# A third score room in the products' two PSUM banks for the first 28 tiles, and the first heads' attended values in the transposes' banks

## The chip, the cores and the metric

The kernel runs on one core of a Trainium2 chip. The metric is device time in microseconds (us) of one execution. The page and the trace used below come from one profiled execution of the kernel before; all times of its instructions are counted from the start of its span.

The engines in this text: PE does matmuls (PEld is its weight load), DVE is the vector engine, ACT the scalar engine, POOL is GpSimd, SP issues most DMAs. Each works through its own instructions in program order and waits on semaphores for the others.

## What is computed

Thresholded softmax attention over 8 batches x 8 heads x 576 positions x 64 values per head, followed by a causal 5-tap convolution that gates a product with one 512x512 matrix, and a product with a second one:

```python
def _attn_ref(q, k, v, tau):
    scale = 1.0 / np.sqrt(q.shape[-1])
    scores = scale * np.matmul(q, k.transpose(0, 1, 3, 2))
    thresh = np.max(scores, axis=-1, keepdims=True) - tau
    scores = np.where(scores >= thresh, scores, -1000000000.0)
    scores = scores - np.max(scores, axis=-1, keepdims=True)
    attn = np.exp(scores)
    attn = attn / (np.sum(attn, axis=-1, keepdims=True) + 1e-09)
    return np.matmul(attn, v)
...
    for k in range(K):
        gate_pre += conv_w[k][None, None, :] * xp[:, k:k + S, :]
    gate = 1.0 / (1.0 + np.exp(-gate_pre))
    val = x @ w_val
    return (gate * val @ w_out)
```

## The kernel before

Two heads make one job, four jobs a batch, 32 jobs in all. A job's scores are made in nine tiles of up to 128 query rows by 576 keys: four row blocks for each head, and one tile that holds the 64 left-over rows of both heads. That makes 288 tiles. Each fp32 operand of the scores and of the two big products is split into a high and a low float32r part, so a score tile is 4 matmuls (`KH,Q` and `KL,Q` for two column halves of 288), the mixed tile 6 (`kh,bdq`, `kl,bdq`).

One tile goes through these steps: PE makes the scores `s` (L498); DVE takes the row maximum into `nm` (L502); ACT makes `e` = exp (L508) and the threshold in `nm` (L510); DVE compares, multiplies and sums into `pp` or `pl` (L524). Then POOL or ACT divides by the sum (L554, L550), PE transposes `pp` in 128x128 pieces into `tp` (L604), ACT copies `tp` to `T` (L615), and once a half of a job's rows is there, PE attends (`acc<-T,v`, L643 and L650) and ACT copies the attended values to `xT` (L658). The convolution's taps run on POOL (L693) and DVE (L700).

When a batch's four jobs are done, its products follow: for each of 2 matrices, 4 blocks of output rows and 2 column halves (320 and 256 wide), twelve matmuls sum into one bank `acc` (L742), that is 16 products or 192 matmuls a batch. A product with the first matrix is read from its bank by DVE (`g`, L769); one with the second by ACT (`o`, L807). These reads are called evacuations below, and so is ACT's copy to `xT`.

At the start the two matrices come in as 64-bit words and DVE, ACT and POOL rebuild them in 16 pieces (L222 to L268) between the first tiles.

PSUM has eight banks, and the kernel gives out all of them: `r_s` two score rooms of two banks each, `r_tp` two banks for transposes, and `r_acc` two banks, which attended values and products share. A `Rooms` object is a list of free buffers; a step that needs one takes it, and the step that is done with it gives it back.

The order of the instructions on every engine is made before the kernel runs: each step is an `op` with a due number (in tiles), a cost and the rooms that it takes and gives; `carry_out` (L140) goes through them on a clock of its own and writes each instruction down at the moment when its engine would begin it. The semaphore waits are not part of this plan. They are added as the instructions are written down: an instruction that reads or writes a buffer waits for the earlier instructions of other engines that wrote or read that buffer.

```python
    r_s = Rooms(ps_s, 2, [P, 2, 512], F32, "s")
    r_tp = Rooms(ps_t, 2, [P, 512], F32, "tp")
    r_acc = Rooms(ps_a, 2, [P, 512], F32, "acc")
```

So each of the two `acc` banks is a buffer of its own, `acc0` and `acc1`.

Of the kernel before, what the change touches and what calls it, by code (L numbers as in the profile page):

```python
# [10 lines left out]
F32 = mybir.dt.float32  # L11
# [4 lines left out]
ALU = mybir.AluOpType  # L16
# [5 lines left out]
DIVIDE = ("ACT",)  # L22
DUE = (8, 8, 8)
PACE_M = 0.17
# [3 lines left out]
def tile_thresholded_attention_gated_mix(  # L28
# [213 lines left out]
    class Words:  # L242


        def __init__(self, u, name, w, c, d0, before):
            due = u * 3.0 - 4
# [33 lines left out]
    def subtract(due, n, get, after, takes=(), gives=()):  # L280


        w = n // 2
        for cols in (slice(0, w), slice(w, n)):
            def run(cols=cols):
                dst, whole, high = get()
                nc.gpsimd.tensor_sub(dst[:, cols], whole[:, cols], high[:, cols].bitcast(F32))  # L287

            cost = w * 0.00237 + 0.04
            after = [op("POOL", due, cost, cost + 0.1, run, after, takes)]  # L290
            takes = ()
        after[0].gives = list(gives)
        return after[0]


    class Job:


        def __init__(self, i, b, g, at):
            self.i, self.b, self.g, self.at = i, b, g, at  # L300
            due = at - 9

            def fetch_v():
                self.v = r_v.take()
                nc.sync.dma_start(self.v, vs[b, g])

            self.got_v = op("SP", at - 3, 0.5, 3.6, fetch_v, takes=[r_v])
            if i == 0:
                self.load_at_once()
            else:  # L310
                self.prepare(due)

        def prepare(self, due):
# [28 lines left out]

            def scale_q():
                nc.gpsimd.tensor_scalar(self.q_r, self.q_r, sc, 0.0, op0=ALU.mult, op1=ALU.add)
# [5 lines left out]
            scaled = op("POOL", due, 0.75, 0.86, scale_q, [got_q])  # L350
            high = op("ACT", due + 1, 0.58, 0.76, high_q, [scaled], [r_qh])
            low = subtract(due + 2, S, low_q, [high], [r_ql], [(r_qr, lambda: self.q_r)])
# [94 lines left out]
    class Tile:  # L447
        def __init__(self, k, t, h, qc, grp):
# [21 lines left out]
            if TH == "ACT":  # L470
                after = [op("ACT", k - DUE[1], 0.83, 1.0, self.weigh, [largest], [r_e])]
            else:
                after = [
                    op("ACT", k - DUE[1], 0.64, 0.78, self.weigh, [largest], [r_e]),
                    op("DVE", k - 9, 0.13, 0.13, self.level, [largest]),
                ]
# [29 lines left out]
        def weigh(self):  # L506
            self.e = r_e.take()
            nc.scalar.activation(self.e, self.s[:, :, :HS], AF.Exp, bias=self.nm[:, 0:1])  # L508
            if TH == "ACT":
                nc.scalar.activation(  # L510
                    self.nm[:, 1:2], self.nm[:, 0:1], AF.Identity, bias=less, scale=-1.0
                )

# [16 lines left out]
    class Group:  # L530
# [5 lines left out]
        def turned(self, k):  # L536
# [4 lines left out]
            add = op("POOL", k - 4, 0.2, 0.33, lambda: nc.gpsimd.tensor_scalar(  # L541
                sums(), sums(), 1.0, 1e-9, op0=ALU.mult, op1=ALU.add), [self.kept])
            inv = op("DVE", k - 4.9, 0.08, 0.33, lambda: nc.vector.reciprocal(ri(0, n), sums()), [add])  # L543
# [15 lines left out]
            for i in range(n):  # L559
                divided.append(op(  # L560
                    "POOL", k - 4 + 0.1 * i, 0.74, 0.82, divide(i, "POOL"), [inv],
# [3 lines left out]
            if self.both:  # L565
                divided.append(op("POOL", k - 4, 0.21, 0.3, lambda: spread(
# [3 lines left out]
            for c0, m in parts:  # L570
# [3 lines left out]
                    "PE", k - 3 + 0.1 * c0, 0.109 * m, 0.109 * (m - 1) + 0.35, self.turn(c0, m),  # L574
# [5 lines left out]
                if not half.begun:  # L580
                    takes, half.begun = [r_T], True
                out.append(op(
                    "ACT", k - 3 + 0.1 * c0, cost, cost + 0.17, self.copy(c0, m), [turn, *half.room], takes,
# [47 lines left out]
    class Half:  # L631
# [4 lines left out]
        def attended(self, k):  # L636
# [3 lines left out]
            def attend():  # L640
                acc = self.acc = r_acc.take()
# [25 lines left out]
            t.got_x = op("ACT", k - 4, cost, cost + 0.2, evacuate, after, [r_xT] if j == 0 else [],  # L667
                         [(r_acc, lambda: self.acc)])
# [185 lines left out]
    for t in jobs:  # L854
# [16 lines left out]
        convolve(t, batch, len(tiles))  # L871
        if t.g == NP - 1:
            last = products(batch, len(tiles) + 4.0, last)
# [44 lines left out]
```

## Time and profile before

| | us |
|---|---|
| median of 3 runs | 766.35 (765.61 to 766.81) |
| the profiled execution | 766.39 |
| its span | 764.6 |
| last score matmuls (`s`, L498) in the chain that ended last | 717.92 |
| last stretch of attended values (`acc<-T,v`, L650) in that chain | 729.80 |

The span is 1.79 us shorter than the profiled execution's own time. How to read the views quoted later: the page's second part cuts the span into 40 slices of 19.1 us and gives each engine's busy tenths; the chain of waits goes back from the last instruction to whatever released it; a table by stretch gives the busy time of each engine in a stretch, with the number of instructions in brackets, and the TensorE clock that was granted (PEclk); the groups give the busy time and the mean nanoseconds of one instruction, then the idle time just before them; the timeline gives start, length, engine and line, with the idle time before and its releaser in brackets.

### The profile page before, as it was taken

To read this page: it belongs to the slowest core of one execution; us is meant where nothing else is said; L and a number is where in the kernel's file an instruction comes from. 1 tells how busy PE (TensorE), PEld (TensorE's weight loads), DVE (VectorE), ACT (ScalarE), POOL (GpSimd) and SP (SyncE) were. 2 spreads that over 40 slices of the span, in tenths; PEclk is the share of its full clock that TensorE was granted. 3 is DMA by queue.
4 is the path that set the end of the run, shared out by engine and by line. 5 is a ranking of instruction groups with operands and counts; after the bars stand their busy time and mean duration, and the time that the engine had idled before them with its cause. 6 is when DMAs were issued, how large, how long until landed. Compare 5 with 4: busy or idle time off the path is not lost.

```text
span 764.6 us, 15851 instructions
## 1 busy us (share of the span) xinstructions
PE 714.2 (93%) x5216; PEld 602.7 (79%) x5216; DVE 617.5 (81%) x1308; ACT 640.9 (84%) x1469; POOL 544.1 (71%) x885
## 2 busy tenths in 40 slices
PE   3687889979999999999999999999999999999997
PEld 3465557767788888888888888888888888888897
DVE  5878999989888878888888787888778988888630
ACT  5788987888889989989998898899889898988832
POOL 3677777778778867787678776688668876775431
PEclk9989999999999999999999999999999999999999
DMA  6746635344665556555555456455455455540001
GB/s 186 182 127 162 168 106 121 109 116 122 177 169 135 129 145 155 154 120 127 141 141 130 124 141 171 123 130 151 123 141 135 125 147 156 141 107 20 32 32 63
DMA packets 51890, 99.05 MB, mean 130 GB/s; under 512 B 9056, under 2 KB 9056, under 8 KB 51808
## 3 DMA queue, kind: packets, MB, share of 16 engines
q1 hardware_dynamic: 51488, 97.47, 49.0%
q8 instruction: 42, 0.69, 0.4%
q10 hardware_dynamic: 320, 0.56, 0.3%
q14 instruction: 40, 0.33, 0.1%
HBM read 35.74 MB, written 9.44 MB: 59 GB/s over the span
## 4 chain that ended last, share of the span: by engine, by line
PE 71%; DVE 8%; ACT 7%; POOL 6%; DMA 4%; issue 3%; SPq 1%; POOLq 0%; ACTq 0%
PE acc L742 20%; PE s L498 17%; PE acc L650 15%; PE tp L604 14%; PE acc L643 4%; DVE nm L502 3%; DMA q_r<-qT 2%; DVE pp L524 2%; ACT e L508 2%; ACT T L615 1%; DVE pre L700 1%; POOL pp L554 1%; POOL xl L287 1%; DMA KL<-kl 1%; POOL gl L287 1%
## 5 line engine op out<-in xcount | busy, mean ns | idle before, releaser
L502 DVE TENSOR_REDUCE nm<-s 128x1 f32<-128x576 f32 x288 | 215.8, 753 | 54.0 <-PE s L498 50.4
L508 ACT ACTIVATE e<-s,nm 128x576 f32<-128x576 f32 x288 | 215.5, 748 | 25.1 <-DVE nm L502 13.0
L524 DVE SCALAR_TENSOR_TENSOR pp<-s,nm,e 128x576 f32<-128x576 f32 x256 | 207.3, 813 | 35.1 <-ACT nm L510 31.7
L615 ACT COPY T<-tp 128x384 f32<-128x384 f32 x384 | 175.3, 487 | 27.6 <-PE tp L604 26.0
L604 PE MATMUL tp<-ident,pp 128*128 128x128 f32 x1152 | 182.3, 277 | 13.0 <-POOL pp L554 6.6
L498 PE MATMUL s<-KH,Q 128*128 128x288 f32 x512 | 162.1, 332 | 19.2 <-DVE Q L434 8.8
L554 POOL TENSOR_SCALAR pp<-pp,sums 128x576 f32<-128x576 f32 x174 | 142.5, 824 | 36.5 <-DVE sums L543 25.2
L604 PEld LDWEIGHTS tp<-ident,pp 128*128 128x128 f32 x1152 | 139.3, 142 | 23.2 <-POOL pp L554 10.1
L498 PE MATMUL s<-KL,Q 128*128 128x288 f32 x512 | 145.9, 299 | 0.7 <-DMA KL<-kl 0.7
L650 PE MATMUL acc<-T,v 128*64 128x256 f32 (+1 forms) x1024 | 138.3, 412 | 0.0
L498 PEld LDWEIGHTS s<-KH,Q 128*128 128x128 f32 x512 | 99.2, 194 | 43.3 <-DVE pp L524 13.8
L700 DVE SCALAR_TENSOR_TENSOR pre<-xT,cw,pre 128x576 f32<-128x576 f32 x128 | 119.2, 931 | 11.1 <-POOL pre L693 11.0
L650 PEld LDWEIGHTS acc<-T,v 128*64 128x64 f32 x1024 | 67.8, 136 | 62.9 <-issue 24.9
L498 PEld LDWEIGHTS s<-KL,Q 128*128 128x128 f32 x512 | 99.1, 194 | 0.9 <-DMA KL<-kl 0.9
L510 ACT ACTIVATE nm<-nm,less 128x1 f32<-128x1 f32 x288 | 85.0, 295 | 0.0
L742 PE MATMUL acc<-gl,woh 128*128 128x320 f32 (+1 forms) x256 | 78.1, 305 | 4.1 <-POOL gl L287 4.1
L742 PE MATMUL acc<-xl,wvh 128*128 128x320 f32 (+1 forms) x256 | 78.7, 307 | 2.6 <-POOL xl L287 2.5
L541 POOL TENSOR_SCALAR sums<-sums 128x2 f32<-128x2 f32 (+1 forms) x160 | 47.5, 297 | 45.5 <-DVE pp L524 33.2
L742 PE MATMUL acc<-gh,woh 128*128 128x320 f32 (+1 forms) x256 | 78.9, 308 | 0.7 <-ACT o L807 0.7
L742 PE MATMUL acc<-xh,wvl 128*128 128x320 f32 (+1 forms) x256 | 79.3, 310 | 0.0
L742 PE MATMUL acc<-xh,wvh 128*128 128x320 f32 (+1 forms) x256 | 78.4, 306 | 0.7 <-DVE g L769 0.5
L742 PE MATMUL acc<-gh,wol 128*128 128x320 f32 (+1 forms) x256 | 78.4, 306 | 0.0
(79 smaller groups left out, 1273.9 us busy)
## 6 DMA issues: line engine op xcount, KB each, us to landing
KH<-kh SPq DMA_DIRECT2D x124, 144.0 KB, 2.5
KL<-kl SPq DMA_DIRECT2D x124, 144.0 KB, 3.2
k_r<-kT SPq DMA_DIRECT2D x32, 320.0 KB, 3.7
v<-vs SPq DMA_DIRECT2D x32, 320.0 KB, 3.0
q_r<-qT SPq DMA_DIRECT2D x32, 288.0 KB, 2.9
outT<-o SPq DMA_DIRECT2D x32, 288.0 KB, 2.2
Q<-qh SPq DMA_DIRECT2D x62, 128.0 KB, 2.3
Q<-ql SPq DMA_DIRECT2D x62, 128.0 KB, 2.5
```

The lines of the kernel that those rows point to most:

```text
L498: nc.tensor.matmul(s[:, a, :HS], w, m, start=i == 0, stop=i == len(terms) - 1)
L502: nc.vector.tensor_reduce(self.nm[:, 0:1], self.s[:, :, :HS], axis=AX.XY, op=ALU.max, negate=True)
L508: nc.scalar.activation(self.e, self.s[:, :, :HS], AF.Exp, bias=self.nm[:, 0:1])
L510: nc.scalar.activation(self.nm[:, 1:2], self.nm[:, 0:1], AF.Identity, bias=less, scale=-1.0)
L524: nc.vector.scalar_tensor_tensor(grp.p[:, i * S : (i + 1) * S].rearrange("p (a f) -> p a f", a=2), self.s[:, :, :HS], self.nm[:, 1:2], self.e,
L541: add = op("POOL", k - 4, 0.2, 0.33, lambda: nc.gpsimd.tensor_scalar(sums(), sums(), 1.0, 1e-9, op0=ALU.mult, op1=ALU.add), [self.kept])
L554: nc.gpsimd.tensor_scalar(v, v, ri(i), 0.0, op0=ALU.mult, op1=ALU.add)
L604: nc.tensor.transpose(tp[:, i * P : (i + 1) * P], self.p[:, k0 : k0 + P], ident)
L615: nc.scalar.copy(T[:, c0 : c0 + n, self.off : self.off + P], tp[:, 0 : n * P].rearrange("p (c q) -> p c q", q=P),)
L650: nc.tensor.matmul(acc[hs, :w], t.v[:, c0 : c0 + D], T[:, h * NKC + c, :], start=False, stop=c == NKC - 1, skip_group_check=True,)
L700: nc.vector.scalar_tensor_tensor(cv, t.xT[:, i : i + S], cw[:, g, i : i + 1], cv, op0=ALU.mult, op1=ALU.add)
L742: nc.tensor.matmul(taken[name, e, j][:, :w], wt[:, c, c0 : c0 + P], moving(c, i)[:, hs], start=n == 0, stop=n == NM - 1,)
```

## The change

The two `acc` banks become one buffer `[P, 2, 512]`, of the same shape as a score room. Until tile 28 it is a third score room. When it is given back after tile 28's scores have been written down (`retired` isn't empty any more), it is not a score room any longer: its two halves, views of the one buffer, go to `r_acc` as two rooms. The attended values of the first batch's heads, up to tile 31, take their bank from `r_tp` instead of `r_acc`.

```diff
+EXTRA = 28
...
+    class Scores(Rooms):
+        def __init__(self, *args):
+            super().__init__(*args)
+            self.extra = None
+
+        def give(self, room, when):
+            if self.extra is not None and room is self.extra and retired:
+                self.extra = None
+                for i in range(2):
+                    r_acc.give(room[:, i, :], when)
+            else:
+                super().give(room, when)
+
+    retired = []
+    r_s = Scores(ps_s, 2, [P, 2, 512], F32, "s")
-    r_s = Rooms(ps_s, 2, [P, 2, 512], F32, "s")
     r_tp = Rooms(ps_t, 2, [P, 512], F32, "tp")
-    r_acc = Rooms(ps_a, 2, [P, 512], F32, "acc")
+    r_acc = Rooms(ps_a, 1, [P, 2, 512], F32, "acc")
+    if EXTRA:
+        r_s.extra = r_acc.take()
+        r_s.give(r_s.extra, 0.0)
...
         def multiply(self):
             t, h, qc = self.t, self.h, self.qc
             s = self.s = r_s.take()
+            if self.k >= EXTRA:
+                retired.append(self.k)
...
             def attend():
-                acc = self.acc = r_acc.take()
+                acc = self.acc = rooms.take()
...
+            rooms = r_tp if EXTRA and t.b == 0 and k < EXTRA + 4 else r_acc
-            made = op("PE", k - 2, cost, cost + 0.2, attend, [t.got_v, *self.copies], [r_acc], gives)
+            made = op("PE", k - AHEAD_A, cost, cost + 0.2, attend, [t.got_v, *self.copies], [rooms], gives)
```

The rest of the diff turns numbers into constants of the same value (`AHEAD_D = 4`, `AHEAD_T = 3`, `AHEAD_A = 2`, `AHEAD_J = 9`, `CONVERT = (3.0, -4)`, `LATE_M = 4.0`) and adds ways that are switched off (`SUB`, `QS`, `level_act`).

The plan gives another order from the first tiles to the end of the program. In the rows below, `s0`, `s1` and `acc0`, `acc1` are buffers of scores and of products, the brackets name the semaphore that a row waits for (DVE_49, Activation_49, Pool_49 and PE_49 count the instructions of an engine, DMAHW a DMA queue's), and a plain number behind x says how many equal rows follow. In the changed kernel L498 is L553, L604 is L664, L643 and L650 are L703 and L710, L742 is L803.

PE at the very start, before: the last row of tile 1 (counted from 0), and tile 2.

```order
L498 MATMUL s1_102<-KL0_119,Q0_115 128x288
L498 MATMUL s0_101<-KH0_117,Q0_115 128x288 [waits DVE_49]
L498 MATMUL s0_101<-KL0_119,Q0_115 128x288
L498 MATMUL s0_101<-KH0_117,Q0_115 128x288
L498 MATMUL s0_101<-KL0_119,Q0_115 128x288
```

The same place in the changed kernel: the last row of tile 1, tile 2, and the start of tile 3.

```order
L553 MATMUL s1_102<-KL0_118,Q0_114 128x288
L553 MATMUL acc0_105<-KH0_116,Q0_114 128x288
L553 MATMUL acc0_105<-KL0_118,Q0_114 128x288
L553 MATMUL acc0_105<-KH0_116,Q0_114 128x288
L553 MATMUL acc0_105<-KL0_118,Q0_114 128x288
L553 MATMUL s0_101<-KH0_116,Q0_114 128x288 [waits DVE_49]
```

Tile 2 waited for DVE to be done with tile 0's room; now it goes to `acc0` and waits for nobody, and tile 3 is the first that waits for a room.

PE at the second job, before (its operands `KH1`, `KL1` and `Q1` come from DMAs): tile 10, a piece of transposing, and the start of tile 11.

```order
L498 MATMUL s0_101<-KH1_118,Q1_116 128x288 [waits DMAHW5_49,DMAHW4_49,DMAHW6_49,DMAHW2_49,DVE_49]
L498 MATMUL s0_101<-KL1_120,Q1_116 128x288 [waits DMAHW7_49,DMAHW0_49]
L498 MATMUL s0_101<-KH1_118,Q1_116 128x288
L498 MATMUL s0_101<-KL1_120,Q1_116 128x288
L604 MATMUL tp1_104<-ident_96,pp2_131 128x128 [waits Activation_49,Pool_49]
L604 MATMUL tp1_104<-ident_96,pp2_131 128x128 x2
L498 MATMUL s1_102<-KH1_118,Q1_116 128x288 [waits DMAHW6_49,DMAHW3_49,DVE_49]
```

The changed kernel: tile 10, and tile 11 behind it.

```order
L553 MATMUL s1_102<-KH1_117,Q1_115 128x288 [waits DMAHW3_49,DMAHW7_49,DMAHW2_49,DVE_49]
L553 MATMUL s1_102<-KL1_119,Q1_115 128x288 [waits DMAHW4_49,DMAHW1_49]
L553 MATMUL s1_102<-KH1_117,Q1_115 128x288
L553 MATMUL s1_102<-KL1_119,Q1_115 128x288
L553 MATMUL acc0_105<-KH1_117,Q1_115 128x288 [waits DMAHW4_49,DMAHW0_49,DVE_49]
L553 MATMUL acc0_105<-KL1_119,Q1_115 128x288 [waits DMAHW5_49,DMAHW2_49]
L553 MATMUL acc0_105<-KH1_117,Q1_115 128x288
L553 MATMUL acc0_105<-KL1_119,Q1_115 128x288
```

Tile 11 follows tile 10 with no transposes between, in the third room. SP's DMAs for this job moved too: the first two `KL1` copies stand ahead of the `Q1` copies now, where they stood behind them.

PE in the last batch's products, before: the end of one product (256 wide, in `acc1`), and the start of the next (320 wide, in `acc0`).

```order
L742 MATMUL acc1_106<-gl3_165,woh_99 128x256
L742 MATMUL acc1_106<-gh3_161,wol_100 128x256
L742 MATMUL acc0_105<-gh0_158,woh_99 128x320 [waits Activation_49]
L742 MATMUL acc0_105<-gl0_162,woh_99 128x320
L742 MATMUL acc0_105<-gh0_158,wol_100 128x320
L742 MATMUL acc0_105<-gh1_159,woh_99 128x320
```

The changed kernel, at the same two products:

```order
L803 MATMUL acc0_105<-gl3_164,woh_99 128x256
L803 MATMUL acc0_105<-gh3_160,wol_100 128x256
L803 MATMUL acc0_105<-gh0_157,woh_99 128x320
L803 MATMUL acc0_105<-gl0_161,woh_99 128x320
L803 MATMUL acc0_105<-gh0_157,wol_100 128x320 [waits Activation_49]
L803 MATMUL acc0_105<-gh1_158,woh_99 128x320
L803 MATMUL acc0_105<-gl1_162,woh_99 128x320
```

The wait for ACT stood at a product's first matmul; it stands at its third now, and both products' rows name one buffer. Over the whole program, of the 1536 rows of products 62 waited for DVE or ACT before, 50 of them at a product's first row; now 163 wait, 16 of them at a first row. On the other side, 115 of the 128 evacuations of products now wait, by the value of PE's semaphore, for a matmul that stands behind the last one of their own product and belongs to the buffer's other half; before, no evacuation waited for more than its own product's last matmul. The evacuation is itself what a later matmul into the other half waits for.

More of the change, by code (lines that the diff above doesn't have):

```diff
@@ L22 @@
 DIVIDE = ("ACT",)
+SUB = False
+EXTRA = 28
+QS = False
 DUE = (8, 8, 8)
+AHEAD_D = 4
+AHEAD_T = 3
+AHEAD_A = 2
+AHEAD_J = 9
+LATE_X = 0
+LATE_M = 4.0
+CONVERT = (3.0, -4)
 PACE_M = 0.17
@@ L176, in carry_out @@
         assert not any(open_ops.values()), "some operations can never begin"
-    r_s = Rooms(ps_s, 2, [P, 2, 512], F32, "s")
-    r_tp = Rooms(ps_t, 2, [P, 512], F32, "tp")
-    r_acc = Rooms(ps_a, 2, [P, 512], F32, "acc")
+    class Scores(Rooms):
[11 more added lines that the diff above has]
+    r_s = Scores(ps_s, 2, [P, 2, 512], F32, "s")
+    r_tp = Rooms(ps_t, 2, [P, 512], F32, "tp")
+    r_acc = Rooms(ps_a, 1, [P, 2, 512], F32, "acc")
+    if EXTRA:
+        r_s.extra = r_acc.take()
+        r_s.give(r_s.extra, 0.0)
+    else:
+        accs = r_acc.take()
+        for i in range(2):
+            r_acc.give(accs[:, i, :], 0.0)
     r_kr = Rooms(raw, 1, [P, SK], F32, "k_r")
@@ L284, in subtract, with run @@
         for cols in (slice(0, w), slice(w, n)):
-            def run(cols=cols):
+            def run(engine, cols=cols):
                 dst, whole, high = get()
-                nc.gpsimd.tensor_sub(dst[:, cols], whole[:, cols], high[:, cols].bitcast(F32))
+                engine.tensor_sub(dst[:, cols], whole[:, cols], high[:, cols].bitcast(F32))
             cost = w * 0.00237 + 0.04
-            after = [op("POOL", due, cost, cost + 0.1, run, after, takes)]
+            fast = w * 0.00116 + 0.07
+            after = [op(
+                "POOL", due, cost, cost + 0.1, lambda run=run: run(nc.gpsimd), after, takes,
+                other=[("DVEp", fast, fast + 0.12, lambda run=run: run(nc.vector))] if SUB else [],
+            )]
             takes = ()
@@ L341, in low_q, with high_scaled, low_scaled @@
                 return self.ql, self.q_r, self.qh
+            def high_scaled():
+                self.qh = r_qh.take()
+                nc.scalar.mul(self.qh, self.q_r, sc)
+            def low_scaled():
+                self.ql = r_ql.take()
+                nc.vector.scalar_tensor_tensor(
+                    self.ql, self.q_r, sc, self.qh.bitcast(F32), op0=ALU.mult, op1=ALU.subtract
+                )
             def scale_q():
@@ L472, in __init__ @@
             else:
+                ways = {"ACT": (0.19, 0.33, self.level_act), "DVE": (0.13, 0.2, self.level)}
+                first, *rest = TH
                 after = [
                     op("ACT", k - DUE[1], 0.64, 0.78, self.weigh, [largest], [r_e]),
-                    op("DVE", k - 9, 0.13, 0.13, self.level, [largest]),
+                    op(first, k - 8.5, *ways[first], [largest], other=[(w, *ways[w]) for w in rest]),
                 ]
@@ L512, in weigh, with level_act @@
                 )
+        def level_act(self):
+            nc.scalar.activation(
+                self.nm[:, 1:2], self.nm[:, 0:1], AF.Identity, bias=less, scale=-1.0
+            )
         def level(self):
@@ L540, in turned @@
             ri = lambda i, m=1: self.sums[:, 2 + i : 2 + i + m]
-            add = op("POOL", k - 4, 0.2, 0.33, lambda: nc.gpsimd.tensor_scalar(
+            add = op("POOL", k - AHEAD_D, 0.2, 0.33, lambda: nc.gpsimd.tensor_scalar(
                 sums(), sums(), 1.0, 1e-9, op0=ALU.mult, op1=ALU.add), [self.kept])
-            inv = op("DVE", k - 4.9, 0.08, 0.33, lambda: nc.vector.reciprocal(ri(0, n), sums()), [add])
+            inv = op("DVE", k - AHEAD_D - 0.9, 0.08, 0.33, lambda: nc.vector.reciprocal(ri(0, n), sums()), [add])
             divided = []
@@ L565, in turned @@
             if self.both:
-                divided.append(op("POOL", k - 4, 0.21, 0.3, lambda: spread(
+                divided.append(op("POOL", k - AHEAD_D, 0.21, 0.3, lambda: spread(
                     self.p[:, S : S + SL], self.p[:, S - SL : S]), divided))
@@ L582, in turned @@
                 out.append(op(
-                    "ACT", k - 3 + 0.1 * c0, cost, cost + 0.17, self.copy(c0, m), [turn, *half.room], takes,
+                    "ACT", k - AHEAD_T + 0.1 * c0, cost, cost + 0.17, self.copy(c0, m), [turn, *half.room], takes,
                     [(r_tp, lambda c0=c0: self.tp[c0])],
@@ L663, in attended @@
                 gives.append((r_v, lambda: t.v))
-            made = op("PE", k - 2, cost, cost + 0.2, attend, [t.got_v, *self.copies], [r_acc], gives)
+            made = op("PE", k - AHEAD_A, cost, cost + 0.2, attend, [t.got_v, *self.copies], [rooms], gives)
             cost = 0.31 if j == 0 else 0.255
             after = [made] if j == 0 else [made, t.got_x]
-            t.got_x = op("ACT", k - 4, cost, cost + 0.2, evacuate, after, [r_xT] if j == 0 else [],
-                         [(r_acc, lambda: self.acc)])
+            t.got_x = op("ACT", k - AHEAD_A - 2, cost, cost + 0.2, evacuate, after, [r_xT] if j == 0 else [],
+                         [(rooms, lambda: self.acc)])
     class Batch:
@@ L870, in tile_thresholded_attention_gated_mix @@
             half.attended(len(tiles) - 1)
-        convolve(t, batch, len(tiles))
+        convolve(t, batch, len(tiles) + LATE_X)
         if t.g == NP - 1:
-            last = products(batch, len(tiles) + 4.0, last)
+            last = products(batch, len(tiles) + LATE_M, last)
     carry_out()
```

18 lines of the change are left out of this document (11 added, 7 removed).

## The prediction

> **What bounds the kernel now.** I read the page first, then the table by stretch, then the groups, and last the timeline at the places that the change touches.
>
> ```profile
> PE 714.2 (93%) x5216; PEld 602.7 (79%) x5216; DVE 617.5 (81%) x1308; ACT 640.9 (84%) x1469; POOL 544.1 (71%) x885
> PE   3687889979999999999999999999999999999997
> DVE  5878999989888878888888787888778988888630
> PE acc L742 20%; PE s L498 17%; PE acc L650 15%; PE tp L604 14%; PE acc L643 4%; DVE nm L502 3%; DMA q_r<-qT 2%; DVE pp L524 2%; ACT e L508 2%; ACT T L615 1%; DVE pre L700 1%; POOL pp L554 1%; POOL xl L287 1%; DMA KL<-kl 1%; POOL gl L287 1%
> ```
>
> The two rows of tenths show two regimes. In the first eight slices or so (some 150 us) PE is not full; from there it stands at 9 to the end. The chain of waits agrees: its five largest lines are PE's own matmuls, together 70%.
>
> ```profile
> 20.00:40.00 20.00, 13.65 (x79) 9.56 (x78) 15.68 (x36) 15.01 (x36) 13.94 (x25) 0.92 0.72 174
> 40.00:60.00 20.00, 16.43 (x105) 12.16 (x104) 16.75 (x42) 17.84 (x44) 14.78 (x26) 0.91 0.58 156
> 80.00:100.00 20.00, 17.43 (x121) 12.28 (x121) 18.93 (x43) 18.19 (x44) 15.82 (x27) 1.00 0.58 148
> 300.00:400.00 100.00, 99.98 (x755) 84.99 (x754) 82.54 (x175) 90.75 (x209) 74.30 (x118) 1.00 0.54 138
> 600.00:700.00 100.00, 100.00 (x763) 86.94 (x762) 85.71 (x181) 90.22 (x209) 72.75 (x116) 1.00 0.48 123
> ```
>
> The columns behind the stretch's length are PE, PEld, DVE, ACT and POOL. From 20 to 60 us DVE is idle 4.32 + 3.25 = 7.57 us; from 80 to 100 it is the full one (18.93 of 20). From 300 on PE is full (99.98 and 100.00 of 100), while DVE has some 15% and ACT 10% to spare. So an idle stretch of DVE that is saved early is worth its length to the end, and one that PE gets late costs its length. The change does the one to the first 28 tiles and the other to everything behind them.
>
> **The early part: what the third room brings.**
>
> ```profile
> DVE nm L502 <- PE s L498: 7.6, 10, 1.9
> PE tp L604 <- ACT T L615: 3.4, 5, 1.2
> DVE pp L524 <- ACT nm L510: 3.3, 7, 1.0
> PE s L498 <- DVE pp L524: 3.1, 5, 2.0
> ```
>
> These are waits between 8 and 80 us (us in total, times, longest). DVE waited 7.6 us for scores. A further room can take away part of that and no more; where the changed order reaches tile 33, DVE has done the same number of maxima, comparisons, word steps and taps as before, so nothing else is saved ahead of it.
>
> ```profile
> 35.95 0.76 DVE L502 TENSOR_REDUCE nm<-s 128x1 f32<-128x576 f32 x1 [1.90 <-PE s L498]
> 35.99 0.86 POOL L287 TENSOR_TENSOR kl<-k_r,kh 128x320 fp32r<-128x320 f32 x1 [2.97 <-DMA KL<-kl]
> 37.67 0.90 PE L604 MATMUL tp<-ident,pp 128*128 128x128 f32 x3 [1.76 <-POOL pp L554]
> 39.57 0.76 DVE L502 TENSOR_REDUCE nm<-s 128x1 f32<-128x576 f32 x1 [1.69 <-PE s L498]
> ```
>
> Nearly half of the 7.6 us is in two waits, at tiles 10 and 11. Tile 10 waited for its data, the last KL copy. Tile 11 waited for a chain: POOL's split of the next job's keys stood ahead of the division, waited for the same copy, the division came late, the transposes waited for it, and tile 11's scores stood behind them on PE. In the changed order no transposes stand between, so the 1.69 us go; the first KL copies stand earlier in SP's queue, ahead of the Q copies, so I give tile 10 back about 1.3 us, with DMA landing as the next to be late. Another 1 us I take for the room waits of tiles 2 to 8, where ACT's `nm` is late next. That sums to 1.69 + 1.3 + 1 = 4 us. Against it stands the second edit: seven attended values hold a transposing bank, and each delays the next transposes by at most the copy that frees it (L658 below, 0.42 us), 7 x 0.42 = 3 us, in a stretch where PE has room; I take nothing for it. Bounds of the early part: 7.6 us gained, 3 us lost. Taken: **-4 us**.
>
> **The late part: what sharing one buffer costs.** From tile 28 on, both banks of products belong to one buffer, and the waits in the built program go by the buffer. An evacuation of one half waits for the matmuls into the other half that were written down ahead of it, and the next matmul into the other half waits for that evacuation. Where PE could run on into the second bank, it now stops for a round trip. The last products show its price.
>
> ```profile
> 743.26 0.28 PE L742 MATMUL acc<-xh,wvl 128*128 128x256 f32 x1
> 743.38 0.31 PE L742 MATMUL acc<-xh,wvh 128*128 128x320 f32 x1
> 743.53 0.31 PE L742 MATMUL acc<-xl,wvh 128*128 128x320 f32 x1
> 743.58 0.42 DVE L769 SCALAR_TENSOR_TENSOR g<-pre,acc 128x256 f32<-128x256 f32 x1 [0.83 <-PE acc L742]
> 743.67 0.31 PE L742 MATMUL acc<-xh,wvl 128*128 128x320 f32 x1
> ```
>
>
> A product ends with the matmul at 743.26 (its end, 743.54, is followed by DVE's evacuation 0.04 later), and PE is already two matmuls into the next, one each 0.147 us. In the changed program the evacuation waits for the second of them, and the third waits for the evacuation. So: the second ends at 743.53 + 0.31 = 743.84; DVE begins at 743.88 and ends at 744.30; then PE is released.
>
> ```profile
> 31.89 0.47 ACT L615 COPY T<-tp 128x384 f32<-128x384 f32 x1
> 32.42 0.55 PE L604 MATMUL tp<-ident,pp 128*128 128x128 f32 x3 [0.41 <-ACT T L615]
> 49.37 0.42 PE L742 MATMUL acc<-xl,wvh 128*128 128x320 f32 x1 [1.20 <-POOL xl L287]
> 49.62 0.29 PE L498 MATMUL s<-KH,Q 128*128 128x288 f32 x1
> ```
>
> The release takes 0.06 us (31.89 + 0.47 = 32.36 to 32.42). A matmul after a wait has its weight load beside it, not ahead of it: the next one begins 0.25 us after it (49.37 to 49.62) in place of 0.15, another 0.10. So the third matmul begins at 744.36, not 743.67, and what follows is 0.69 + 0.10 = 0.79 us late, here with a 256-wide `g`.
>
> ```profile
> L769 DVE SCALAR_TENSOR_TENSOR g<-pre,acc 128x320 f32<-128x320 f32 x32 | 15.3, 480 | 5.2 <-PE acc L742 5.2
> L769 DVE SCALAR_TENSOR_TENSOR g<-pre,acc 128x256 f32<-128x256 f32 x32 | 13.3, 414 | 3.5 <-PE acc L742 3.3
> L807 ACT ACTIVATE o<-acc 128x320 f32<-128x320 f32 x32 | 14.0, 439 | 6.7 <-PE acc L742 6.4
> L807 ACT ACTIVATE o<-acc 128x256 f32<-128x256 f32 x32 | 12.7, 396 | 4.9 <-PE acc L742 4.9
> L658 ACT COPY xT<-acc 128x320 f32<-128x320 f32 x32 | 13.5, 423 | 10.4 <-PE acc L650 10.1
> ```
>
> Averaged over both widths, `g` takes 0.447 and `o` 0.417 us, so a round trip is 0.81 us for `g` and 0.78 for `o`: (0.31 - 0.147) + 0.04 + the evacuation + 0.06 + 0.10.
>
> How many are paid is counted in the changed order. 122 of the 128 evacuations of products have a later matmul waiting for them. In 75 (42 of `g`, 33 of `o`) nothing stands on PE between the matmul that the evacuation waits for and the one that waits for the evacuation: 42 x 0.81 + 33 x 0.78 = 60 us. In 29 some scores or transposes stand between, on average 0.43 us of them at their spacing, which leaves 10.6 us. In 18 there is enough to hide all of it. The copies to `xT` are mostly followed by a dozen other matmuls; they add 2.4 us. Together **+73 us**. Twenty of the 122 lie behind the last score tile, where nothing else could fill PE:
>
> ```profile
> 731.68 11.88 PE acc L742 x89
> ```
>
> Here PE made 89 matmuls of products in a row, 0.133 us each. Seven product ends lie in such a run, and I expect seven stops of 0.8 us in it.
>
> What hides of the rest: PE is full in the rows from 300 on, so a stop is not taken from idle time. Some stops will fall where PE would have waited anyway; from 200 to 300 it is idle for 2.2 us (97.82 of 100 busy, quoted below), and the early rows have more. I take 3 us for that. On the other side, DVE and ACT now stand at an evacuation until PE gets there, with `L502` or `L508` of the next tile queued behind it, and their 10 to 15% to spare must carry that. I take no loss for it, and put it among the rivals.
>
> Sum: 766.39 - 4 + 73 - 3 = **832 us**, against the profiled execution's own 766.39 (the span's 764.6 and 1.79 around it), which lies 0.04 above the median of the runs.
>
> Bounds. Low: without the weight load's 0.10, price 0.7 and the early gain at 7.6: 75 x 0.7 + 8 + 2 = 62, 766.4 - 7.6 + 62 - 3 = 818. High: early loss 3, no overlap, and in each of the 104 paid stops the evacuating engine is 0.15 us late on average (half of ACT's 0.3 us threshold step): 766.4 + 3 + 73 + 16 = 858.
>
> **The rivals.**
>
> *Half of it is absorbed: 797 us, chance 0.12.* The plan's order fixes who stands behind whom, not the times; where PE runs behind DVE and ACT by more than a round trip, the matmul ahead is late, the evacuation follows at once, and a later wait of PE for scores' rooms or transposes is shortened by what was lost. For it: PE's busy time has modelled ends, so 99.98 is not proof of no gaps. Against it: the run of 89 at 0.133 us has none. Price: 766.4 - 4 + 35 = 797.
>
> *The engines catch on each other: 890 us, chance 0.09.* An evacuation waits on ACT behind an exp or in front of one; when PE's stop comes while ACT is in the middle of it, the stop grows by up to one such step.
>
> ```profile
> 43.88 0.75 ACT L508 ACTIVATE e<-s,nm 128x576 f32<-128x576 f32 x1
> ```
>
> At 0.75 us more in three quarters of 104 stops: 832 + 58 = 890. For it: ACT is at 90%. Against it: once PE is slower by 8%, ACT is at 83%.
>
> *Not slower: 762 us, chance 0.03.* The stops never bite, since by the time PE comes to the waiting matmul the evacuation is over; what is left is the early gain. That decides only if some 0.8 us of other matmuls stand between on PE; in 75 cases none do. Price 766.4 - 4 = 762.
>
> *The clock falls: 935 us, chance 0.04.* Many short stops might let the granted clock drop.
>
> ```profile
> 30.00:40.00 10.00, 5.89 (x34) 4.72 (x31) 6.08 (x14) 5.77 (x14) 5.36 (x9) 0.83 0.77 189
> 100.00:110.00 10.00, 7.18 (x49) 4.92 (x47) 9.55 (x22) 7.71 (x20) 7.32 (x11) 1.00 0.51 145
> 200.00:300.00 100.00, 97.82 (x728) 82.70 (x726) 83.49 (x176) 89.73 (x207) 80.88 (x132) 1.00 0.56 143
> ```
>
> The clock was 0.83 in a stretch with PE busy for 5.89 of 10 us, and 1.00 in one with 7.18 of 10. With stops of 0.8 us in 9% of the time PE stays above both. If it did fall to 0.83 over the 500 us from 200 to 700, PE's work there would take 500 / 0.83 - 500 = 102 us more: 832 + 102 = 934. The Trainium skill, "TensorE: Matmul & The Clock Gate", section "A second HAM failure mode: psum-queue depth-cycling", speaks against this change: a kernel that cycles through PSUM banks can make PE idle so often for so short that its clock gate swings between half and full. By that rule the rival's 934 would be the time; the trace doesn't agree at this share of idling, since the stretch at 7.18 kept 1.00, so the chance stays small.
>
> **How the numbers follow.** The forecast, 832 us, has the rest, 0.72. Its own range is 818 to 858. The range that should hold 8 in 10 also takes in the lower rival's upper part, down to 800, and the upper rival's lower part, up to 865: the tails left out on both sides are some 0.1 each. A difference under 0.2% (1.5 us) can't be told from none by a measurement of this kernel. Faster by more: 0.03; within: 0.01; slower by more: 0.96.
>
> **What would show it.** On the page of the changed kernel: products' groups (L803) with some 60 us of idle time before them, released by DVE's `g` (L830) and ACT's `o` (L868); PE at some 88% with digits of 8 from slice 8 on; in the last 30 us stops of 0.7 to 0.8 us at each product. The span behind the last score tile should grow by 20 x 0.8 = 16 us. For the early part: the maximum of tile 11 at some 36 us in place of 39.57, and DVE's waits for scores to 80 us at 3 to 4 us in place of 7.6. The prediction is wrong if L803 waits for its evacuations for less than 30 us in all, or if the time up to tile 33 differs by more than 8 us.

## The result, and the profile after

| | median us (lowest to highest) | ratio to before, 95% interval |
|---|---|---|
| before, 4 runs beside the changed kernel | 766.58 (765.61 to 766.82) | |
| the changed kernel, 4 runs | 835.85 (833.59 to 837.63) | 1.0905 (1.0869 to 1.094) |

The changed kernel is 9% slower; the profiled execution has a span of 835.7 us. Ratios here and below leave out two slow executions far above the others: one of the kernel before at 902.6 us (granted clock 0.755), and one of the kernel before with doubled evacuations (an experiment below) at 2424.58 us (clock recorded as 1.00, cause open). First its page: busy times, the tenths of PE and of its clock, and the shares of the chain of waits.

```profile
PE 741.6 (89%) x5216; PEld 609.4 (73%) x5216; DVE 618.7 (74%) x1308; ACT 649.0 (78%) x1472; POOL 540.3 (65%) x882
PE   4776878979989999999999998999999999999876
PEclk9999899999999999999999999999999999999999
PE acc L803 24%; PE s L553 16%; PE acc L710 14%; PE tp L664 13%; PE acc L703 3%; DVE g L830 3%; ACT e L563 3%; ACT o L868 2%; DVE pp L584 2%; DVE nm L557 1%; DVE pre L761 1%; ACT T L675 1%; ACT nm L565 1%; ACT pp L610 1%; POOL pp L614 1%
```

The two kinds of evacuation, `g` (L830) and `o` (L868), stand in the chain with 3% and 2%; before, neither was among the lines shown. The granted clock shows 9 in all slices but one. PE's waits over the whole run (us in total, times, longest):

```profile
PE acc L803 <- DVE g L830: 26.9, 49, 1.9
PE acc L803 <- ACT o L868: 18.0, 40, 0.6
```

Before, each of these two was a single wait of 0.5 and 0.7 us. Now 89 stops show 44.9 us of idle time. The table by stretch says where:

```profile
300.00:400.00 100.00, 94.84 (x692) 78.99 (x692) 76.41 (x162) 84.00 (x192) 68.94 (x111) 1.00 0.50 129
500.00:600.00 100.00, 93.63 (x672) 78.56 (x671) 74.84 (x158) 80.65 (x185) 65.87 (x110) 0.98 0.46 120
600.00:700.00 100.00, 94.48 (x685) 77.88 (x685) 75.41 (x160) 83.19 (x189) 68.44 (x114) 1.00 0.50 128
```

From 300 to 400 and from 600 to 700 us PE now does 692 and 685 matmuls in place of 755 and 763, some 8 to 10% fewer, and DVE and ACT slow down with it. From 200 to 800 us there are 9 to 14 of the stops in every 100 us, and 13 more in the last 36. In the last 60 us the stops stand alone, and the chain of waits shows them one after another (start, length):

```profile
816.31 1.75 PE acc L803 x12
818.07 0.02 issue
818.09 0.39 ACT o L868
818.48 0.04 issue
818.52 1.98 PE acc L803 x12
820.51 0.03 ACTq L868
820.53 0.04 issue
820.58 0.45 ACT o L868
821.02 0.04 issue
821.07 1.75 PE acc L803 x12
```

Twelve matmuls, then ACT's evacuation, then twelve matmuls. Two products take 821.07 - 816.31 = 4.76 us. The timeline of the same place has the matmuls 0.118 and 0.147 us apart (256 and 320 wide), so without stops it would be 12 x (0.118 + 0.147) = 3.18 us. Each stop costs (4.76 - 3.18) / 2 = 0.79 us. Only a part of it is idle time, which the timeline gives in brackets:

```profile
817.60 0.31 PE L803 MATMUL acc<-gh,woh 128*128 128x320 f32 x1
817.75 0.31 PE L803 MATMUL acc<-gl,woh 128*128 128x320 f32 x1
818.52 0.42 PE L803 MATMUL acc<-gh,wol 128*128 128x320 f32 x1 [0.47 <-ACT o L868]
818.78 0.31 PE L803 MATMUL acc<-gh,woh 128*128 128x320 f32 x1
```

The wait stands at the third matmul of the 320-wide product, as in the order. It begins 818.52 - 817.75 = 0.77 us after the second, and 0.47 of that is shown as idle; the rest lies in the modelled length of the matmul ahead and in the slower start (0.42 instead of 0.31 long, the next one 0.26 behind it instead of 0.147). This is why PE's busy time rose too, from 714.2 to 741.6 us, by 27.4. Its idle time over the whole span rose from 764.6 - 714.2 = 50.4 to 835.7 - 741.6 = 94.1 us, by 43.7. The two together are the 71.1 us by which the span grew.

The last score matmul ends at 773.61 (718.72 before), so what lies behind it grew from 764.6 - 718.72 = 45.9 to 835.7 - 773.61 = 62.1 us.

The early part. The maximum of tile 11 begins at 36.99 us in place of 39.57, that of tile 26 at 68.66 in place of 78.74, and that of tile 27 at 80.22 in place of 80.15: a lead of 10 us is gone in one tile. Between the scores of these two tiles PE never waits for more than 0.58 us; it does transposes and attended values that the order puts there. What follows is a long wait, ahead of tile 28. SP's queue and PE's timeline there:

```profile
73.19 6.32 SPq L284 DMA_DIRECT2D o<-w_val  x2
79.56 1.11 SPq L448 DMA_DIRECT2D Q<-ql  x2
```

```profile
83.40 0.58 PE L553 MATMUL s<-KH,Q 128*128 128x288 f32 x1 [4.89 <-DMA o<-w_val]
```

The fourth job's last copies of `Q` stand in SP's queue behind two loads of matrix words, and the second of these waits for its buffer. (PE doesn't read `o`: the releaser in the row is the one that the profile saw last.) The table by stretch shows the same of DVE, which was the full engine there before (18.93 of 20):

```profile
80.00:100.00 20.00, 14.48 (x90) 12.41 (x91) 16.23 (x37) 16.17 (x38) 15.18 (x27) 0.83 0.65 174
```

From 20 to 80 us DVE's idle time fell from 9.41 to 5.99 us, so 3.4 us were saved; from 80 to 100 us it rose from 1.07 to 3.77, and 2.7 of them were lost again (the granted clock was 0.83 there, 1.00 before). At tile 33 the changed kernel is 0.40 us ahead (94.08 against 94.48).

### The profile page after: what moved, and what is told of

The parts are those of the page before. It is cut to its first block, busy times and chain, and to the rows that moved or that the text cites. A ratio compares the mean times of both kernels' runs of the same rounds, so it can differ in the third digit from the quotient of the medians.

```text
span 835.7 us, 15859 instructions
## 1 busy us (share of the span) xinstructions
PE 741.6 (89%) x5216; PEld 609.4 (73%) x5216; DVE 618.7 (74%) x1308; ACT 649.0 (78%) x1472; POOL 540.3 (65%) x882
## 4 chain that ended last, share of the span: by engine, by line
PE 71%; ACT 10%; DVE 9%; issue 4%; POOL 3%; DMA 2%; SPq 0%; POOLq 0%; ACTq 0%; DVEq 0%
PE acc L803 24%; PE s L553 16%; PE acc L710 14%; PE tp L664 13%; PE acc L703 3%; DVE g L830 3%; ACT e L563 3%; ACT o L868 2%; DVE pp L584 2%; DVE nm L557 1%; DVE pre L761 1%; ACT T L675 1%; ACT nm L565 1%; ACT pp L610 1%; POOL pp L614 1%
## 5 line engine op out<-in xcount | busy, mean ns | idle before, releaser
L557 DVE TENSOR_REDUCE nm<-s 128x1 f32<-128x576 f32 x278 | 208.0, 753 | 71.4 <-PE s L553 67.8
L584 DVE SCALAR_TENSOR_TENSOR pp<-s,nm,e 128x576 f32<-128x576 f32 x246 | 199.0, 812 | 43.5 <-ACT nm L565 40.6
L563 ACT ACTIVATE e<-s,nm 128x576 f32<-128x576 f32 x278 | 207.4, 746 | 26.3 <-DVE nm L557 15.5
L664 PE MATMUL tp<-ident,pp 128*128 128x128 f32 x1152 | 181.7, 277 | 8.8 <-ACT T L675 4.6
L553 PE MATMUL s<-KH,Q 128*128 128x288 f32 x492 | 156.3, 332 | 28.0 <-DVE pp L584 10.9
L664 PEld LDWEIGHTS tp<-ident,pp 128*128 128x128 f32 x1152 | 139.7, 142 | 18.4 <-ACT T L675 6.2
L553 PE MATMUL s<-KL,Q 128*128 128x288 f32 x492 | 140.8, 300 | 0.0
L553 PEld LDWEIGHTS s<-KH,Q 128*128 128x128 f32 x492 | 95.8, 195 | 50.8 <-DVE pp L584 15.0
L710 PE MATMUL acc<-T,v 128*64 128x256 f32 (+1 forms) x912 | 122.9, 412 | 0.0
L710 PEld LDWEIGHTS acc<-T,v 128*64 128x64 f32 x912 | 60.4, 136 | 55.5 <-issue 21.9
L553 PEld LDWEIGHTS s<-KL,Q 128*128 128x128 f32 x492 | 96.0, 195 | 0.0
L803 PE MATMUL acc<-gh,wol 128*128 128x320 f32 (+1 forms) x256 | 81.4, 318 | 12.0 <-ACT o L868 9.5
L803 PE MATMUL acc<-xh,wvl 128*128 128x320 f32 (+1 forms) x256 | 80.9, 316 | 11.6 <-DVE g L830 11.0
L803 PE MATMUL acc<-xl,wvh 128*128 128x320 f32 (+1 forms) x256 | 79.6, 311 | 6.9 <-DVE g L830 5.9
L803 PE MATMUL acc<-xh,wvh 128*128 128x320 f32 (+1 forms) x256 | 79.2, 309 | 6.9 <-DVE g L830 6.6
L803 PE MATMUL acc<-gh,woh 128*128 128x320 f32 (+1 forms) x256 | 79.9, 312 | 5.7 <-ACT o L868 4.5
L803 PE MATMUL acc<-gl,woh 128*128 128x320 f32 (+1 forms) x256 | 79.4, 310 | 4.2 <-ACT o L868 2.6
```

The source lines that it names most:

```text
L553: nc.tensor.matmul(s[:, a, :HS], w, m, start=i == 0, stop=i == len(terms) - 1)
L557: nc.vector.tensor_reduce(self.nm[:, 0:1], self.s[:, :, :HS], axis=AX.XY, op=ALU.max, negate=True)
L584: nc.vector.scalar_tensor_tensor(grp.p[:, i * S : (i + 1) * S].rearrange("p (a f) -> p a f", a=2), self.s[:, :, :HS], self.nm[:, 1:2], self.e,
L664: nc.tensor.transpose(tp[:, i * P : (i + 1) * P], self.p[:, k0 : k0 + P], ident)
L710: nc.tensor.matmul(acc[hs, :w], t.v[:, c0 : c0 + D], T[:, h * NKC + c, :], start=False, stop=c == NKC - 1, skip_group_check=True,)
L803: nc.tensor.matmul(taken[name, e, j][:, :w], wt[:, c, c0 : c0 + P], moving(c, i)[:, hs], start=n == 0, stop=n == NM - 1,)
```

## The experiments

Each ratio is against runs of the kernel before on the same chip. For pieces that were measured on different chips, ratios are subtracted and multiplied by 767 us.

**The shared buffer alone.** Every engine's order is that of the kernel before; only the two banks are halves of one buffer.

```diff
-EXTRA = 28
+EXTRA = 0
```

> The changed kernel with EXTRA = 0: no third score room, attended values in the products' banks, and the order of every engine is that of the kernel before; only the two product banks are halves of one buffer. If the shared buffer is the cause (the stops of some 0.8 us at each evacuation), this alone costs what the whole change costs: 830 to 845 us. If the new order, the third room or the transposes' banks are the cause, it stays near the kernel before: 765 to 780 us.

Measured: 837.81 us (836.52 to 840.47), ratio 1.091 (1.0889 to 1.0932), 70 us over the kernel before. The sharing makes the whole loss by itself, without a third room and without a moved instruction.

**The changed order with two buffers.** At tile 28 the shared buffer's pool is closed, and the products get two buffers of one bank each in the same place.

```diff
...
+                guard.__exit__(None, None, None)
+                ps_b = ctx.enter_context(tc.tile_pool(name="ps_b", bufs=1, space=bass.MemoryType.PSUM))
                 for i in range(2):
-                    r_acc.give(room[:, i, :], when)
+                    r_acc.give(ps_b.tile([P, 512], F32, name=f"own{i}"), when)
```

> The changed kernel in its own order, with the third room until tile 28, but at that point the buffer is closed and two buffers of one bank each are opened in its place, so each half is waited for by itself. If the shared buffer is the cause: 762 to 770 us (the early lead of 10 us at tile 26 is gone by tile 28, so I expect about the time of before, 766). If the order or the banks of the attended values are the cause: above 800 us.

Measured: 766.03 us (763.9 to 769.28, 8 runs), ratio 0.9975 (0.9956 to 0.9994). Of all its waits of products only this row is left:

```profile
PE own L806 <- POOL gl L323: 1.2, 1, 1.2
```

So the sharing costs (1.0905 - 0.9975) x 767 = 71 us. And the rest of the change, the third room, the order and the transposes' banks together, gains 0.25% or 1.9 us (0.5 to 3.4). The lead of the third room goes at the same place: tile 26 at 68.77, tile 27 at 80.34 us.

The Trainium skill, "Perfetto Trace Analysis", section "Matmuls", says that independent groups of matmuls should rotate through different PSUM banks so that one group's evacuation overlaps the next one's matmuls. Both kernels rotate through the same two banks; with two buffers no wait of a product for an evacuation shows, with one buffer 89 do. Here the rule holds only where each bank is a buffer to whoever writes the waits.

**Evacuations twice.** Each `g` and each `o` is written twice in a row, in the changed kernel, in the kernel before, and (as a better control) in the one with two buffers.

```diff
...
-                        nc.scalar.mul(o[f][:, hs], taken["wo", f, j][:, 0 : hs.stop - hs.start], 0.5)
+                        for _ in range(2):
+                            nc.scalar.mul(o[f][:, hs], taken["wo", f, j][:, 0 : hs.stop - hs.start], 0.5)
```

> The changed kernel with every evacuation of a product written twice (the same result). If PE stops for a round trip that contains the evacuation, each of about 104 paid stops grows by its length, 0.447 us for g and 0.417 for o: 836 + 40 to 48 = 876 to 884 us. If PE's stops are something else (the waits are over by the time PE comes), the 57 us of added work on DVE and ACT, which are idle for 22 to 26% there, hides: 836 to 845 us.

> The same doubling in the kernel before, as a control: with two buffers PE runs on into the other bank while the evacuation lasts, so little is added: 766 to 774 us. If the added work itself costs time on DVE and ACT: 785 us or more, and then the doubling in the changed kernel says less.

> The kernel with two banks of its own for the products (order of the changed kernel), and every g and o evacuation written twice. It is the control for the doubled evacuations in the shared buffer (897.0 us against 837.8 or so for single ones, +60), better than the doubled kernel before, whose profiled execution was not usable. Theory stops (every evacuation is on PE's path in the shared buffer, and only there): here the doubled work costs what DVE and ACT have no room for, some 128 x 0.38 = 49 us of work spread over both engines, of which about the 32 us that the doubled kernel before lost shows again: 796 to 802 us, with waits of products for DVE or ACT at first matmuls only. Rival (doubling costs nothing on own banks, so all 60 us are the stops): 766 to 772 us.

Measured: 897.04 us in the shared buffer (1.1672; 1.165 to 1.1693), 799.6 in the kernel before (1.0409; 1.0389 to 1.0429; three executions), 794.43 with two buffers (1.0343; 1.0297 to 1.0389; two executions only). All three expectations were missed. The shared buffer lost 59 to 61 us over the changed kernel instead of 40 to 48. The kernel before lost 31 instead of at most 8, so the other case of its expectation came (785 us or more). With two buffers the time lies 1.6 us under the range of 796 to 802. Doubled evacuations cost 28 to 31 us even where PE doesn't stop for them, so the time of the first kernel can't be read alone. PE's own waits in it can:

```profile
PE acc L803 <- DVE g L831: 52.4, 52, 2.3
PE acc L803 <- ACT o L870: 40.7, 52, 1.0
```

These are 104 stops and 93.1 us of idle time, against 89 stops and 44.9 us with single evacuations: 48.2 us more, where 40 to 48 was expected of the stops. In the chain of waits near the end, each stop holds both writings (pieces of 0.02 and 0.04 us left out):

```profile
878.41 1.75 PE acc L803 x12
880.18 0.39 ACT o L870
880.59 0.39 ACT o L870
881.03 1.99 PE acc L803 x12
883.04 0.45 ACT o L870
883.51 0.45 ACT o L870
884.00 1.75 PE acc L803 x12
```

Two products take 884.00 - 878.41 = 5.59 us here, against 4.76 with single evacuations: 0.42 more for each stop, the length of one evacuation. So at these stops the whole evacuation lies on PE's path. How the other 11 to 13 us of the 59 to 61 arise was not shown; taking off all of the 28 us that doubling costs with two buffers would leave 31 us for the stops, less than PE's waits show, so not all of it is paid here.

**One bank that the plan knows of.** The shared buffer gives only one half, and a product takes it only when its operands are all there (otherwise a product that has begun could hold the only bank that its own operands need).

```diff
-AHEAD = False
+AHEAD = True
...
-                for i in range(2):
-                    r_acc.give(room[:, i, :], when)
+                r_acc.give(room[:, 0, :], when)
```

> The changed kernel, but at its retirement the shared buffer gives only one of its halves to the products and attended values, and a product takes it only when all its operands are there. So the plan knows that there is one bank, and puts other matmuls between an evacuation and the next product; 124 product rows wait for DVE or ACT, at first matmuls. Theory order (most of the 70 us came from matmuls that the plan wrote down in two halves turn by turn, which in truth exclude each other): the stops while scores still run are covered, what stays is the tail of about 20 products behind the last score at 0.8 us each and a few us: 780 to 795 us. Rival (one bank instead of two is what costs, whether the plan knows it or not): 825 to 850 us.

Measured: 795.75 us (794.37 to 797.81), ratio 1.0362 (1.0328 to 1.0396): just above the range that the order theory gave (780 to 795), far from its rival, and 42 us faster than with two halves. PE's waits for evacuations at the products:

```profile
PE acc L802 <- DVE g L829: 6.5, 10, 1.4
PE acc L802 <- ACT o L867: 6.5, 11, 1.0
```

21 stops and 13 us, in place of 89 and 45, and only 4 of the 21 come ahead of the last score matmul: while scores still run, other matmuls stand between. The last score matmul ends at 732.75 us of a span of 796.0, so the part behind it is 63.3 us: there the loss stays (17 us over before's 45.9). The other 11 of the 28 us over the kernel before were not traced.

The second edit alone, with both halves given:

> The changed kernel with both halves given, in which a product takes its half only when all its operands are there (the second of the two edits of the one-half kernel, without the first). Theory order (the plan still writes two halves turn by turn, so the stops inside products stay; the one-half kernel's 40 us came from the plan's knowing of one bank): 820 to 845 us. Rival (whole products behind ready operands are what made the one-half kernel 40 us faster than the changed one): 790 to 805 us.

Measured: 837.17 us (835.92 to 837.87), ratio 1.0902 (1.0866 to 1.0937), no different from the changed kernel. The 42 us come from the plan's knowing of one bank.

**The lost lead.** Three kernels with two buffers prepare jobs earlier, so that the `Q` copies stand ahead of the word loads; one does it in the kernel before; one keeps the third room longer.

```diff
-AHEAD_J = 9
+AHEAD_J = 10
```

> The kernel with own banks, and the preparation of every job due one tile earlier (10 tiles ahead instead of 9). On SP the fourth job's last copies of Q then stand ahead of the two loads of matrix words that wait for a free buffer. Theory queue (the 10 us lead of the third room at tile 26 is lost because these copies stand behind a waiting load): the 4.8 us wait of PE at tile 27 goes to under 2, tile 33 begins 3 to 8 us earlier than at 94.2 us, and the end 2 to 6 us earlier than with own banks alone: 760 to 764 us. Rival (the words' conversions on DVE and POOL must be done by then anyway, so the lead is given back a few tiles later): 765 to 768 us, tile 60's maximum within 1.5 us of 167.7.

The same edit with 12:

> The same with the preparation of jobs 12 tiles ahead: one of the two word loads goes behind the Q copies too, and the words are converted later. Theory queue: as with 10 tiles, 758 to 764 us. Rival (lead given back to the conversions): 765 to 768 us; and earlier jobs can hold their buffers longer and delay tiles 9 to 18, then 767 to 772 us.

Only the fourth job earlier:

```diff
-            due = at - AHEAD_J
+            due = at - AHEAD_J - (3 if i == 3 else 0)
```

> The kernel with own banks, in which the fourth job alone (tiles 27 to 35) is prepared three tiles earlier; its last copies of Q then stand ahead of both word loads on SP, and all jobs before it are as they were. Theory queue (the lead at tile 26 is lost to the waiting word load alone): PE's 4.8 us wait at tile 27 goes, tile 28's maximum begins at 72 to 78 us instead of 84.7, and the end is 2 to 5 us earlier than own banks alone (ratio to before 0.991 to 0.995). Rival (a lead in tiles is not a lead in work: words and products that are put off have to be done all the same, and PE's work done by 200 us decides): tile 28 earlier as above, but PE's busy time in the first 200 us grows by under 2 us over the 160.0 of own banks, and the ratio stays at 0.996 to 0.999.

The kernel before, with its number there:

```diff
-            due = at - 9
+            due = at - 12
```

> The kernel before with the preparation of jobs 12 tiles ahead instead of 9, and without a third room. Theory (the third room is what makes the earlier preparation of use: own banks with 12 tiles was 0.9956 of before): 0.997 to 1.003 of before. Rival (the earlier preparation is worth those 3 to 4 us by itself, with or without the third room): 0.994 to 0.996.

Two buffers, 12 tiles ahead, and a longer third room:

```diff
-EXTRA = 28
+EXTRA = 36
```

> The best version so far (own banks, jobs 12 tiles ahead), with the third room kept to tile 36 instead of 28, and attended values in the transposes' banks up to tile 39. Theory (the room still helps while words are being converted, and products have too little to do before tile 36): 760 to 764 us, ratio 0.990 to 0.995. Rival (the products begin later by those tiles, and transposes wait for their two banks, which attended values hold longer): 765 to 770 us, PE's busy time in the first 200 us under the 163.5 us of 28 tiles.

Measured, with the start of two maxima and PE's busy time in the first 200 us, each from its own profiled execution:

| kernel | tile 28 us | tile 60 us | PE busy to 200 us | span us | ratio (95% interval) |
|---|---|---|---|---|---|
| before | 83.56 | 169.43 | 158.07 | 764.6 | 1 |
| two buffers, 9 tiles ahead | 84.72 | 167.72 | 160.03 | 764.9 | 0.9975 (0.9956 to 0.9994) |
| two buffers, 10 tiles | 74.30 | 168.35 | 161.80 | 767.5 | 1.002 (0.9993 to 1.0047) |
| two buffers, 12 tiles | 71.69 | 158.69 | 163.52 | 760.3 | 0.9956 (0.9939 to 0.9973) |
| two buffers, fourth job early | 73.42 | 163.33 | 154.72 | 771.7 | 1.0074 (1.005 to 1.0097) |
| before, 12 tiles | 82.34 | 165.13 | 164.96 | 760.5 | 0.9959 (0.9936 to 0.9981) |
| two buffers, 12 tiles, room to 36 | 70.35 | 154.29 | 156.51 | 771.0 | 1.0099 (1.0064 to 1.0134) |

The table by stretch has PE's sum in its second column; of the kernel before with 12 tiles ahead, of the fourth job early, and of two buffers with 10 tiles:

```profile
0.00:200.00 200.00, 164.96 (x1091) 130.27 (x1092) 173.31 (x386) 169.27 (x388) 147.40 (x251) 0.97 0.59 150
```

```profile
0.00:200.00 200.00, 154.72 (x1016) 121.58 (x1017) 170.85 (x379) 162.33 (x372) 148.95 (x253) 0.96 0.57 145
```

```profile
0.00:200.00 200.00, 161.80 (x1033) 126.61 (x1034) 170.78 (x382) 168.22 (x385) 142.98 (x241) 0.94 0.56 146
```

With 10 tiles (769.47 us) and with the fourth job alone (773.23), the times of both theories were missed: neither gained, though with 10 tiles the rival's sign came, tile 60 within 1.5 us of 167.7. With 12 tiles (764.21) the time lies at the upper edge of the queue theory's range; in the kernel before with 12 tiles (762.99) the rival held. The longer room (774.22) is later than either of its theories, with PE's busy time under 163.5 us as its rival said. The wait of 4.8 us that two expectations place at tile 27 stands ahead of tile 28's scores (4.76 us with two buffers), and once the copies stand ahead no wait of PE there is longer than 1.6 us. The queue theory was right about tile 28 (71 to 74 us once the copies stand ahead) and wrong about the end: the kernel with only the fourth job early is 10 us ahead of the kernel before at tile 28, 6 us ahead at tile 60, and ends 0.7% later. A lead in tiles is not a lead in work. PE's busy time to 200 us ranks the ends better: the two with the most (164.96 and 163.52) have the shortest spans, the two with the least (154.72 and 156.51) the longest. The kernel with 10 tiles doesn't fit (161.80, yet 767.5). Its granted clock was the lowest of the seven in these 200 us (0.94, against 0.96 and 0.97), so its busy time holds longer matmuls; in number of matmuls it is behind (1033, against 1038 with 9 tiles ahead and 1066 with 12). That this is the whole reason was not tested. PE makes the same matmuls in all of them, so what isn't done by then is done later; for the longer room, that tiles are early and PE's work is late means that products were put off (120 of their matmuls by 200 us, against 153 with the room to 28).

The kernel before with 12 tiles ahead and no third room gains as much as the one with third room and 12 tiles (0.9959 and 0.9956). So of these versions' gain the third room has no part that shows. Both beat the kernel before by 0.4%, with intervals that leave out 1, and the changed one by far.

## Why the prediction was right, and where its terms were off

The forecast of 832 us lies 3.85 below the median of 835.85; the prediction's direction, its likeliest case and its mechanism held.

- *Sharing, +73 us less 3 of overlap:* right. The sharing costs 70 us by itself and 71 in the changed order. The price of a stop was 0.78 us for `o`, and the last products, which `o` reads, show 0.79. The number of stops was 75 in full and 29 in part, 104 in all; the profile shows 89, and 104 with doubled evacuations. Whether 3 us were hidden is not shown by itself.
- *What L803 would show, some 60 us of idle time:* too much, 44.9 us. The price was right, but the profile books only 0.5 us of each stop as idle and the rest as busy matmul. The prediction's own working had the parts (a weight load of 0.10, an end that is modelled) and forgot them when it named what the page would show. For the same reason PE's digits stay at 9 in most slices, where 8 was said; its share is 89%, where 88% was said.
- *The tail, +16 us:* right, 62.1 - 45.9 = 16.2.
- *The early part, -4 us:* of the right sign, mis-sized. The changed order with two buffers gives 1.9 us of gain (0.5 to 3.4), and the changed kernel was 0.40 us ahead at tile 33. Its parts: tile 11 at 36.99 (some 36 was said). Tile 10, which was to come 1.3 us earlier, begins at 36.32 in place of 35.95; it no longer waits, but DVE does other work ahead of it. DVE's waits for scores between 8 and 80 us, 7.6 before, are these now:

```profile
DVE nm L557 <- PE s L553: 5.1, 4, 3.2
DVE nm L557 <- PE acc L553: 0.2, 1, 0.2
```

  That is 5.3 us, where 3 to 4 was said; 3.2 of it is one wait. The step that failed is the one that counted the early part as DVE's saved idle time up to tile 33, with nothing late behind it. To 80 us 3.4 us were saved, close to the 4, but then tile 28 waited for the fourth job's copies in SP's queue, which the prediction didn't look at, and by 100 us 2.7 of them were lost. Nor was tile 33 the right mark: the kernel with the fourth job early is 8.6 us ahead there (85.93 us) and ends later than before, since work that was put off doesn't show there. Why the end gained 1.9 us and not 4 stays open beyond that.
- *Half absorbed (797):* no. PE is the bound from 200 us on in the kernel before (97.82 of 100 busy from 200, 99.98 from 300), and of 73 us 71 were paid.
- *The engines catch on each other (890):* no. The longest stop for ACT is 0.6 us; of the stops for DVE one is 1.9 us, the others 0.68 at most. ACT fell to 78% busy.
- *Not slower (762):* that is what the change gives with two buffers (766), and only there.
- *The clock falls (935):* no, but for one dip. Of the four stretches of 100 us from 300 on, three show 1.00 and one 0.98, and the mean of the execution is 0.988, against 0.99 before. The dip follows the longest stop, which ends at 522.0 us: from 522 to 526 us the granted clock is 0.57. Whether the stop brought it on was not tested. By the rule of the Trainium skill on cycling through PSUM banks ("TensorE: Matmul & The Clock Gate", "A second HAM failure mode: psum-queue depth-cycling") the clock could have swung all along; with 89 stops at 94 to 95% busy it did not.

## What to carry to other kernels

Two views of one buffer are one buffer to whoever writes the waits: before banks are joined or lent, count for each evacuation which later writes would wait for it, and price a stop at the round trip (here 0.79 us, 0.42 of it the evacuation). If a resource is scarcer than the plan believes, tell the plan: one known bank cost 28 us, two that were secretly one cost 69. And measure an early lead in the work that the bounding engine has done, not in the number of the tile that it has reached; in six of the seven kernels above that told the end, and a tile's number did not.

## What was not expected

Writing each evacuation twice adds 0.43 us to each of 128, spread over two engines that are 81 and 84% busy before. With two buffers it cost 28 us all the same. PE's busy time is 731.6 us there, against 714.2 before, and its product rows hardly wait for evacuations:

```profile
PE tp L667 <- ACT T L678: 4.1, 14, 0.6
PE s L556 <- DVE pp L587: 4.0, 10, 1.0
PE own L806 <- POOL gl L323: 1.2, 1, 1.2
PE own L806 <- ACT gh L850: 0.8, 2, 0.6
PE own L706 <- ACT o L873: 0.5, 2, 0.4
```

These are PE's largest waits from 200 us on in that kernel. They are short stops behind ACT's and DVE's other work, each with a part booked as busy; that they make up the 28 us was not shown.
